# Splitting only the first of seven Fourier products a second time, and giving the projection's operands other buffers

## The chip, the cores and the metric

The kernel runs on one core of one Trainium2 chip. The metric is the device time of one execution in microseconds (us). The engines are named as in the profile: PE is the matrix engine (its weight loads are listed apart as PEld), DVE the vector engine, ACT the scalar engine, POOL the general engine, SP the engine that here issues all transfers between the chip's memory (DRAM) and its buffers (SBUF). PSUM is the memory that matmuls write to, in banks of 128x512 numbers. Each engine and the SP queue work through their instructions in a fixed order; an instruction whose semaphores are not there yet holds up all that stand behind it on that engine.

## The reference

Two independent results stand side by side in the output, both in fp32:

```python
# A: attention with 32 heads of width 32, S = 2048, D = 1024
qkv = x @ wqkv                      # (2048, 1024) @ (1024, 3072)
p = softmax(q @ k^T * 32 ** -0.5)   # per head
a = concat_heads(p @ v) @ wo        # the projection: (2048, 1024) @ (1024, 1024)
# B: Fourier mixing, real part of a two-dimensional transform
u, w = x @ dft_hid_re.T, x @ dft_hid_im.T
b = dft_seq_re @ u - dft_seq_im @ w
out = concatenate([a, b], axis=-1)
```

The kernel may take B in the other order, first over the sequence with the two 2048x2048 matrices (`ct`), then over the hidden dimension (`wd`): the first of these is the "first Fourier stage", `dense1`, the second is `dense2`.

## The kernel before

**Four dense stages and an attention.** The dense stages are the QKV product, `dense1`, `dense2` and the projection (`project`). Each saves multiplications by the scheme of Strassen and Winograd: a product of 2x2 blocks is had from seven block products instead of eight, at the price of sums and differences of operands beforehand and of results afterwards. The seven are numbered 1 to 7. For accuracy every fp32 operand is cut into a high and a low part of a faster format (`halves`: a cast `h`, then a subtraction for `l`), and each term costs three matmuls: hi by hi, lo by hi, hi by lo. One such matmul has 128x128 weights and moves 512 columns.

**dense1.** Its seven products come in the order `OUTER`, each over a quarter of the contraction. A product that is not split (`simple`) has 4x4 blocks of the result with 8 terms of three matmuls each, 384 matmuls; the stationary operand (from `xb`, 8 pieces) is loaded once and held, the moving one (from `ct`, 8 pieces) anew for each of four columns `n`. A product in `SPLIT` is cut into seven once more (`split`): 7 products of 4 blocks with 4 terms, 336 matmuls, but with more sums on DVE and POOL, operands that are written to DRAM and read back (`w_d`), and four tiles of accumulators, buffers 16 to 19. The unsplit products use these four buffers for half of the held pieces. Before, products 1, 2 and 3 are split.

**Operands.** `fetch` loads a quarter of an operand into a ring of six tiles `raw`, a second one into a ring of four tiles `g`, and adds or subtracts on POOL or DVE; a sum that is wanted again is stored. `moving` then makes the two halves in one of the numbered buffers (`slot`): 0 to 11 rotate through all dense stages, 12 to 15 and 20 to 27 belong to the projection once the attention's tiles are given up (`op_pool`), 16 to 19 hold accumulators or held pieces. `CR` is a ring of four tiles `c`, for earlier results that are read back to be added to.

**The order of the work.** A planner in the kernel (class `Plan` and the loop at the end) writes down the order of every engine ahead of time, by costs of its own. The matmuls of the dense stages are a list of fills that PE takes between those of the attention: scores twice per head (`psS`, L1536, for the row maxima and sums; `psT`, L1661, transposed, for the weights) and the product with V (`pd<-pt,vt`, L1691, four narrow matmuls side by side). PE takes a fill if nothing of the attention can run, or if the share of the fills that has been paid is not above the share of the attention that is done:

```python
TO_PAY = sum(x[3] for x in fills[: FILL - RES])       # a fill of a split product counts HEAVY = 1.5
if fill is not None and (not ok or (not first and left <= HB) or paid / TO_PAY <= done / ATT):
```

So the fills are spread over the attention such that the last of `dense2` are left when it ends. While a split product runs, and in the projection, ACT may make the casts as well (`spare[0]`).

**The end.** When the last head is done, its result goes to DRAM (`o_d<-ot`). `behind()` makes buffers 12 to 15 and 20 to 27 wait for the results of all heads, and so do the loads into the rings that `project` uses. Its seven products follow in the order 1, 7, 2, 6, 5, 3, 4, with 8 blocks of 4 terms each (96 matmuls); blocks 0 to 3 of the result use the moving operand `A[p, 0, c]` as stationary one (`J0`), blocks 4 to 7 `A[p, 1, c]` (`J1`), and `wo` is `B[p, c]`. `WHERE` says in which buffers they lie.

Of the kernel before, what the change touches and what calls it, by code (L numbers as in the profile page):

```python
# [8 lines left out]
F32 = mybir.dt.float32  # L9
# [215 lines left out]
def kernel(  # L225
# [38 lines left out]
    def slot(i, shape, dt=F32R):  # L264
        if i < 12:
            return big.tile(shape, dt, name=f"slot{i}", tag=f"slot{i}")
        if i < 16 and "pt2" in late:
            return op_pool().tile(shape, dt, name=f"slot{i}", tag=f"slot{i}")
        if i < 16:
            att()  # L270
            return late["low"].tile(shape, dt, name=f"slot{i}", tag=f"slot{i}")
        if i < 20:
            return run.tile(shape, dt, name=f"slot{i}", tag=f"slot{i}")
        if i < 28:
            op_pool()
            return late["oph"].tile(shape, dt, name=f"slot{i}")
        return vph.tile(shape, dt, name=f"slot{i}")

    parts = ctx.enter_context(tc.tile_pool(name="parts", bufs=1, side="right", reuse_waits="tile"))
# [12 lines left out]
    run = ctx.enter_context(tc.tile_pool(name="run", bufs=1, side="right", reuse_waits="tile"))  # L294
    qk0 = tc.alloc_tile_pool(name="qk0", bufs=1, side="right")
    QS, KS, QX = [qk0.tile([P, S], F32R, name="qs0")], [qk0.tile([P, S], F32R, name="ks0")], []
# [82 lines left out]
    ADD = 0.68  # L379
    SPLIT = (1, 2, 3)  # L380
    HEAVY = 1.5
# [67 lines left out]
    slots = [[] for _ in range(40)]  # L449

    def take_slot(i):
        old, slots[i] = slots[i], []
        return old, slots[i]
# [7 lines left out]
    class Kept:  # L461


        def __init__(self, get):
            self.get, self.made, self.users = get, None, []

    def fetch(shape, terms, store=None, keep=None):

        box = {}
        raws, seconds, tile_of, gate = where[0]  # L470
        rank = seq()
        sign, *first = terms[0]
        loaded = len(first) == 2
        if len(terms) == 1 and not loaded:
# [12 lines left out]
        last = None  # L487
        if loaded:
            last = op("SP", ISSUE, lambda: nc.sync.dma_start(dest(), first[0]), old + first[1] + gate, [users], rank, 256, raws if keep is None else None)
            old = []  # L490
        for sign, *term in terms[1:]:
            other = {}
            if len(term) == 2:
                gold, gusers = seconds.take()

                def load(src=term[0], other=other):
                    other["q"] = tile_of(shape, "g", len(seconds.users))
                    nc.sync.dma_start(other["q"], src)

                q = op("SP", ISSUE, load, gold + term[1] + gate, [gusers], rank, 256, seconds)  # L500
            else:
                other["k"], q, gusers = term[0], term[0].made, term[0].users

            def add(e, sign=sign, other=other, a=None if last is not None else first[0]):
                return (nc.gpsimd if e == "POOL" else nc.vector).tensor_tensor(  # L505
                    out=dest(), in0=dest() if a is None else a.get(), in1=other["q"] if "q" in other else other["k"].get(), op=ALU.add if sign > 0 else ALU.subtract)

            last = op("POOL", SUB, add, old + [first[0].made if last is None else last, q], [users, gusers] + ([first[0].users] if last is None else []),
                      rank, 0, raws if keep is None and last is None else None, other=("DVE", ADD, 20 + rank), two=True)
            old = []  # L510
        if keep is not None:
            keep.made = last
# [80 lines left out]
    class Acc:  # L593
# [5 lines left out]
        def at(self):  # L599
            return self.get()[:, self.half]  # L600
# [564 lines left out]

    OUTER = (1, 5, 2, 6, 7, 4, 3)
    WITHIN = (1, 2, 5, 6, 7, 3, 4)
    DONE_IN = {2: (0, 0), 7: (1, 1), 3: (0, 1), 4: (1, 0)}

    def outer(p, X, Y, to, wrote, neg):  # L1170
# [51 lines left out]
        return finish  # L1222

    def dense1():
        s4 = [[[] for _ in range(2)] for _ in range(4)]
# [11 lines left out]
        cq = lambda e, s, n: (ct[e, s, :, n * NB : n * NB + NB], [])  # L1237
        step = [0]

# [3 lines left out]
        def simple(p):  # L1243
# [11 lines left out]
            for n in range(4):  # L1255
# [15 lines left out]
                for m in range(4):  # L1271
# [4 lines left out]
                    if p == 7 and 3 in SPLIT and m % 2:  # L1276
                        i, k = divmod(2 * n + m // 2, 2)
                        fetch([P, 4, P], [(1, *xq(i, 8 + 4 * k)), (-1, s2_d[i][k], s2[i][k])], (s4_d[i][k], s4[i][k]))

        def split(i):  # L1280
            def base_a(m, k):
# [11 lines left out]
            at = lambda *k: (w_d[k], w[k])  # L1293
            x, y = accs(16) + accs(17), accs(18) + accs(19)
            for j in WITHIN:
                z = step[0]
                step[0] += 1
                A, M = [], {}
                for n in range(2):
                    A.append(piece(split_a(j, lambda r, k: base_a(2 * r + n, k), at(5, n), at(6, n)), at(j, n) if j in (5, 6) else None))  # L1300
                    for c in range(4):
                        M[n, c] = moving((8 * z + 4 * n + c) % 12, split_b(j, lambda k, e: base_b(4 * k + c, 2 * e + n), at(5, n, c), at(6, n, c)),
                                         at(j, n, c) if j in (5, 6) else None)
                for n in range(2):
# [41 lines left out]
    def dense2():  # L1346
# [9 lines left out]
        def load_ab(step, k):  # L1356
            p = ORDER[step]
            AB[step, k] = moving((8 * step + k) % 12, moving_terms(p, lambda r, e: (wd[r, k, :, e * NB : e * NB + NB], []), (t2_d[k], t2[k])),
                                 (t2_d[k], t2[k]) if p == 6 else None)
# [31 lines left out]
    def op_pool():  # L1391
        if "op" not in late:
            late["pt2"].release()
            att().release()
            qk0.release()
            late["atl"].release()
# [4 lines left out]
    def behind():  # L1401

        over.extend(o for h in o_st for o in h)
        for i in (*range(12, 16), *range(20, 28)):
            slots[i] = list(over)
# [5 lines left out]
    def project():  # L1411
# [15 lines left out]
        def b_terms(p, c):  # L1427
# [326 lines left out]
    dense2()  # L1754
    behind()
    project()


# [135 lines left out]
```

## Time and profile before

| | before |
|---|---|
| median of 3 runs | 2948.45 us (2947.95 to 2951.28) |
| the profiled execution | 2951.01 us; its span, first to last instruction, 2949.2 us |
| PE busy | 2919.6 us (99%), 14778 matmuls |
| DVE / ACT / POOL busy | 2311.3 (78%) / 2308.5 (78%) / 1188.9 us (40%) |
| transfers | 665.10 MB, mean 226 GB/s; SP's transfers take 69.5% of the 16 DMA engines' time |
| mean granted PE clock | 0.998 |

A trace's row for a group gives the line, the engine, the operation, and output <- inputs by the program's names. A matmul's record is longer than the step from one to the next (a mean of 390 ns, a step of under 230), since matmuls are pipelined; so the busy share of PE says little, and the count of matmuls in a stretch says more. A row of a table by stretches gives from:to, the length, busy time and count (x) of PE, PEld, DVE, ACT and POOL, then the granted PE clock, the mean busy share of the DMA engines and what they moved in GB/s. A product with V is recorded as two matmuls.

### The profile page before, as it was taken

The numbers are of one execution on the slowest core, as the hardware profiler recorded it, in microseconds if no ns is written. First come the engines' busy times: TensorE is split into PE (matmuls) and PEld (weight loads), VectorE is DVE, ScalarE is ACT, GpSimd is POOL, SyncE is SP. The second block draws the span as 40 slices with busy tenths as digits, with TensorE's granted clock in tenths as the row PEclk, the third lists the DMA queues.
The fourth block names the chain that finished last, engine by engine and source line by source line (L and its number), as shares of the span: only waits on it lengthen the run. The fifth ranks groups of instructions, "written<-read, shape, count | busy, mean of one in ns | idle before, by whom it ended". The sixth has DMA issues, their size and how long they took to land.

```text
span 2949.2 us, 46415 instructions
## 1 busy us (share of the span) xinstructions
PE 2919.6 (99%) x14778; PEld 2117.7 (72%) x14778; DVE 2311.3 (78%) x3127; ACT 2308.5 (78%) x4387; POOL 1188.9 (40%) x929
## 2 busy tenths in 40 slices
PE   9999999999999999999999999999999999999999
PEld 7887777777767677666777777777676677777677
DVE  7778888788888867988777787778877887876385
ACT  5347888888888888889888888898888888887431
POOL 2223335222366622676435342247512664342042
PEclk9999999999999999999999999999999999999999
DMA  9975668676697964989979775468734875663463
GB/s 345 370 239 179 206 189 276 213 239 222 229 294 239 324 199 146 294 256 323 307 234 289 227 235 171 147 197 273 226 101 149 283 231 183 189 189 117 161 207 125
DMA packets 460799, 665.10 MB, mean 226 GB/s; under 512 B 117486, under 2 KB 152046, under 8 KB 460430
## 3 DMA queue, kind: packets, MB, share of 16 engines
q1 hardware_dynamic: 460556, 662.14, 69.5%
q8 instruction: 119, 1.95, 0.3%
q14 instruction: 124, 1.02, 0.1%
HBM read 470.06 MB, written 191.91 MB: 224 GB/s over the span
## 4 chain that ended last, share of the span: by engine, by line
PE 58%; DMA 3%; DVE 2%; ACT 2%; issue 1%; POOL 1%; SPq 0%; DVEq 0%; POOLq 0%; ACTq 0%
PE pd L419 26%; PE psT L1661 10%; PE pd L1691 10%; PE psS L1536 9%; PE psT L419 3%; ACT psS L1545 2%; DMA raw<-in_ct 1%; DVE negm L1542 1%; DVE slot L526 0%; DMA g<-in_xb 0%; ACT pt L1668 0%; DMA g<-t_d 0%; POOL raw L505 0%; DVE slot L529 0%; DMA ks<-qk_d 0%
## 5 line engine op out<-in xcount | busy, mean ns | idle before, releaser
L1542 DVE TENSOR_REDUCE negm<-psS 128x1 f32<-128x1024 f32 x1024 | 1241.4, 1220 | 231.4 <-PE psS L1536 220.2
L1545 ACT ACTIVATE psS<-psS,negm 128x1024 f32<-128x1024 f32 x1024 | 1231.1, 1202 | 76.6 <-DVE negm L1542 75.0
L1668 ACT ACTIVATE pt<-psT 128x512 f32<-128x512 f32 x1656 | 1001.3, 703 | 257.1 <-PE psT L1661 235.3
L419 PE MATMUL pd<-slot,h 128*128 128x512 f32 x2784 | 952.9, 390 | 2.3 <-POOL slot L529 2.1
L1661 PE MATMUL psT<-qs,ks 128*128 128x512 f32 x2048 | 798.0, 395 | 4.1 <-ACT pt L1668 3.9
L505 POOL TENSOR_TENSOR raw<-raw,g 128x512 f32<-128x512 f32 x367 | 476.0, 1305 | 436.2 <-issue 63.1
L529 POOL TENSOR_TENSOR slot<-raw,slot 128x512 fp32r<-128x512 f32 x290 | 374.0, 1297 | 680.0 <-DVE slot L529 199.2
L419 PEld LDWEIGHTS pd<-slot,h 128*128 128x128 f32 x2784 | 523.0, 188 | 110.8 <-POOL slot L529 3.7
L419 PE MATMUL pd<-slot,l 128*128 128x512 f32 x1392 | 543.5, 390 | 1.9 <-DVE l L529 1.6
L1661 PEld LDWEIGHTS psT<-qs,ks 128*128 128x128 f32 x2048 | 382.1, 188 | 158.8 <-issue 44.4
L1536 PE MATMUL psS<-ks,qs 128*128 128x512 f32 x1552 | 476.0, 392 | 7.0 <-ACT psS L1545 7.0
L419 PE MATMUL pd<-slot,slot 128*128 128x512 f32 x1536 | 420.2, 389 | 0.0
L1691 PE MATMUL pd<-pt,vt 128*32 128x512 f32 x3312 | 408.2, 594 | 0.0
L1536 PEld LDWEIGHTS psS<-ks,qs 128*128 128x128 f32 x1552 | 288.2, 188 | 76.9 <-ACT psS L1545 17.4
L419 PEld LDWEIGHTS pd<-slot,slot 128*128 128x128 f32 x1536 | 288.5, 188 | 59.9
L1545 ACT ACTIVATION_READ_ACCUMULATOR psS<-psS,negm 128x1 f32 x1024 | 328.8, 321 | 0.0
L419 PEld LDWEIGHTS pd<-slot,l 128*128 128x128 f32 x1392 | 261.6, 188 | 57.1 <-DVE l L529 2.0
L1668 ACT ACTIVATE ptm<-psT 128x512 f32<-128x512 f32 x392 | 241.8, 710 | 43.8 <-PE psT L1661 40.6
L1691 PEld LDWEIGHTS pd<-pt,vt 128*32 128x32 f32 x3312 | 108.5, 110 | 231.4 <-issue 219.3
L529 POOL TENSOR_TENSOR l<-raw,h 128x512 fp32r<-128x512 f32 x120 | 155.2, 1293 | 276.7 <-PE psT L1661 79.3
L526 DVE CAST slot<-raw 128x512 fp32r<-128x512 f32 x375 | 192.0, 531 | 8.4 <-POOL raw L505 7.6
L1536 PE MATMUL psS<-ks,qx 128*128 128x512 f32 x496 | 150.5, 394 | 3.4 <-ACT psS L1545 3.4
(140 smaller groups left out, 2047.4 us busy)
## 6 DMA issues: line engine op xcount, KB each, us to landing
raw<-in_ct SPq DMA_DIRECT2D x240, 256.0 KB
g<-in_ct SPq DMA_DIRECT2D x168, 256.0 KB
raw<-ut_d SPq DMA_DIRECT2D x112, 256.0 KB
qk_d<-e SPq DMA_DIRECT2D x52, 512.0 KB
qs<-qk_d SPq DMA_DIRECT2D x128, 192.0 KB
ks<-qk_d SPq DMA_DIRECT2D x128, 192.0 KB
c<-xx_d SPq DMA_DIRECT2D x80, 256.0 KB
c<-u_d SPq DMA_DIRECT2D x72, 256.0 KB
```

Of the source, the lines that this page charges most:

```text
L419: nc.tensor.matmul(box["ps"], a[1]((a[0].hi, a[0].lo)[u]()), b[1]((b[0].hi, b[0].lo)[v]()), start=k == 0, stop=k == n - 1)
L505: return (nc.gpsimd if e == "POOL" else nc.vector).tensor_tensor(out=dest(), in0=dest() if a is None else a.get(), in1=other["q"] if "q" i ...
L526: return nc.vector.tensor_copy(hi(), raw())
L529: return (nc.gpsimd if e == "POOL" else nc.vector).tensor_tensor(out=lo(), in0=raw(), in1=f(hi()), op=ALU.subtract)
L1536: nc.tensor.matmul(p[:, i * NB : i * NB + NB], (QX[0] if own else QS[h % 2])[:, qt * P : qt * P + P], KS[h % 2][:, c * 1024 + i * NB : c * ...
L1542: nc.vector.tensor_reduce(out=ST["negm"][:, c, qt : qt + 1], in_=box["p"], axis=AX.X, op=ALU.max, negate=True)
L1545: nc.scalar.activation(box["p"], box["p"], AF.Exp, bias=ST["negm"][:, c, qt : qt + 1], accum_out=ST["sums"][:, c, qt : qt + 1])
L1661: nc.tensor.matmul(box["p"], KS[h % 2][:, t * P : t * P + P], QS[h % 2][:, j * NB : j * NB + NB], start=True, stop=True)
L1668: nc.scalar.activation(box["t"], box["p"], AF.Exp)
L1691: nc.tensor.matmul(po["p"][j * DH : j * DH + DH, :], VT[h][:, k, :], box["t"], start=(k == t0), stop=(k == t), tile_position=(0, j * DH),)
```

## The change

Only product 1 of `dense1` is split; products 2 and 3 become `simple`. The order of the seven products puts 2 ahead of 5. In product 1, for one of the two halves of the columns, four tiles that are needed by inner products 1, 5, 6 and 4 stay in SBUF, in the four tiles of `CR`: each is loaded with a quarter of `ct` and then turned in place into t = q01 - t, t = q11 - t, t = t - q10, instead of being stored and read back; `fetch` learns to take the operands of a subtraction the other way round. The buffers 24 to 27 are no longer given out when the attention's tiles are given up: they become the halves of two tiles that take the place of `qs0` and `ks0`, Q and K of the even heads, which are free when head 30 has had its last scores. Products of the projection are laid out anew (`WHERE`), such that `B[1, c]` goes to the bank of 0 to 11 that `dense2` leaves free and `A[1, 0, c]` to 24 to 27; both are asked for ahead of `behind()`. In the planner's sum `FILL` and in its weights the split products 2 and 3 drop out.

```diff
-        if i < 28:
+        if i < 24:
             op_pool()
             return late["oph"].tile(shape, dt, name=f"slot{i}")
+        if i < 28:
+            return both(i, dt)[:, i % 2 * 2 : i % 2 * 2 + 2]
...
+    def both(i, dt):
+        n, turn = i // 2, turns[i]
+        if whole_of.get(n, (None, None))[0] != turn:
+            whole_of[n] = turn, qk0.tile([P, 4, NB], dt, name=f"both{n}", tag=("qs0", "ks0")[n % 2])
...
-    SPLIT = (1, 2, 3)
+    SPLIT = (1,)
...
     def take_slot(i):
+        if 24 <= i < 28:
+            if i % 2 == 0:
+                first[i] = slots[i] + slots[i + 1]
+            old, slots[i] = first[i - i % 2], []
+            return old, slots[i]
...
-    OUTER = (1, 5, 2, 6, 7, 4, 3)
+    OUTER = (1,2,5,6,7,4,3)
...
+            own = {(1, c): stays() for c in range(4)} if i == 1 else {}
...
+                        t = own.get((n, c))
+                        if t is not None and j in (1, 5, 6, 4):
+                            terms = {1: lambda: [(1, *q(0, 0))], 5: lambda: [(-1, t), (1, *q(0, 1))], 6: lambda: [(-1, t), (1, *q(1, 1))], 4: lambda: [(1, t), (-1, *q(1, 0))]}[j]()
+                            M[n, c] = moving((8 * z + 4 * n + c) % 12, terms, None, t)
...
+        g = [(8 * (steps[0] + 7) + 4 * k) % 12 for k in range(3)]
         WHERE = {
-            1: ([20, 24], 0), 7: ([4, 8], 20), 2: ([0, 4], 24), 6: ([8, 0], 20),
-            5: ([4, 8], 24), 3: ([0, 4], 20), 4: ([8, 0], 24),
+            1: ([24, 20], g[0]), 7: ([g[1], g[2]], 24), 2: ([g[0], g[1]], 20), 6: ([g[2], g[0]], 24),
+            5: ([g[1], g[2]], 20), 3: ([g[0], g[1]], 24), 4: ([g[2], g[0]], 20),
         }
...
+        for i in range(24, 28):
+            slots[i] = [Tops[H - 2][-1], Sops[H - 2][-1]]
         load_b(1)
-        load_a(1, J0 + J1)
+        load_a(1, J0)
+        behind()
+        load_a(1, J1)
```

The built programs show what this does to the order. Counted over the whole program, PE has 96 matmuls more (two products with 384 instead of 336), SP issues 2624 transfers instead of 2840, POOL has 775 instructions instead of 934, DVE 3061 instead of 3129, ACT 3320 instead of 3365.

**The end of the first product, on SP.** Before, loads, second operands (`g`) and stores of sums (`s_d`, `t_d`) for product 5 are issued while the results of product 1 (`xx_d`) are written:

```order
L489 DMA raw<-in_ct 128x512
L514 DMA s_d_0_534<-raw 128x512
L498 DMA g<-in_ct 128x512
L489 DMA raw<-in_xb 128x512
L970 DMA xx_d_0_1_438<-e 128x512
L514 DMA t_d_0_542<-raw 128x512
L498 DMA g<-in_xb 128x512
L514 DMA t_d_1_543<-raw 128x512
```

Now single loads for product 2 stand there:

```order
L994 DMA xx_d_0_1_454<-e 128x512
L511 DMA raw<-in_xb 128x512
L1205 DMA c<-xx_d_0_1_454 128x512
L511 DMA raw<-in_xb 128x512
L994 DMA xx_d_1_1_442<-e 128x512
L511 DMA raw<-in_xb 128x512
L324 DMA ks_333<-qk_d_3_85 96x512
```

The second operands and the stores of product 5 have moved behind product 2, one product further on.

**The end of the attention, on PE.** Here the last block of `dense2` (`slot,h` and `slot,l`) is followed by the projection's first product. Before:

```order
L419 MATMUL psT<-slot_30505,h 128x512
L419 MATMUL psT<-slot_30505,l 128x512
L419 MATMUL psT<-slot_30505,h 128x512
L419 MATMUL psT<-slot_31205,slot_31235 128x512 x3
L419 MATMUL psT<-slot_31211,slot_31257 128x512 x3
L419 MATMUL psT<-slot_31219,slot_31262 128x512 x3
```

Now:

```order
L433 MATMUL psT<-slot_29912,h 128x512
L433 MATMUL psT<-slot_29912,l 128x512
L433 MATMUL psT<-slot_29912,h 128x512
L433 MATMUL psT<-slot_30363,both_30532 128x512 x3
L433 MATMUL psT<-slot_30386,both_30532 128x512 x3
L433 MATMUL psT<-slot_30467,both_30589 128x512 x3
```

The first product reads the new tiles; between the last product with V and this place stand 53 matmuls of `dense2` before, and 91 now.

**The same place on SP.** Before, all of the projection's loads stand behind the store of the last head's result:

```order
L1731 DMA o_d_200<-ot 128x512
L970 DMA out<-e 128x512
L489 DMA raw<-in_wo 128x512 x4
L489 DMA raw<-o_d_193 128x512
L970 DMA out<-e 128x512
```

Now two of the four loads of `wo` stand ahead of it, and the others right behind:

```order
L511 DMA raw<-in_wo 128x512
L994 DMA out<-e 128x512
L1006 DMA c<-u_d_601 128x512
L511 DMA raw<-in_wo 128x512
L1781 DMA o_d_200<-ot 128x512
L511 DMA raw<-in_wo 128x512
L994 DMA out<-e 128x512
L511 DMA raw<-o_d_193 128x512
```

Of the 36 transfers for the projection's first two products, 34 are still issued after the attention.

More of the change, by code (lines that the diff above doesn't have):

```diff
@@ L488, in fetch @@
         if loaded:
-            last = op("SP", ISSUE, lambda: nc.sync.dma_start(dest(), first[0]), old + first[1] + gate, [users], rank, 256, raws if keep is None else None)
+            last = op("SP", ISSUE, lambda: nc.sync.dma_start(dest(), first[0]), old + first[1] + gate, [users], rank, 256, raws if keep is None else keep.ring)
             old = []
@@ L511, in fetch @@
         if keep is not None:
-            keep.made = last
+            keep.made, keep.ring = last, None
         if store is not None:
@@ L1278, in simple, with stays, get @@
                         fetch([P, 4, P], [(1, *xq(i, 8 + 4 * k)), (-1, s2_d[i][k], s2[i][k])], (s4_d[i][k], s4[i][k]))
+        def stays():
+            box = {}
+            def get():
+                if "t" not in box:
+                    box["t"] = sums_pool().tile([P, NB], F32, name="c", tag="c", bufs=NCR)
+                return box["t"]
+            k = Kept(get)
+            old, k.users = CR.take()
+            k.users.extend(old)
+            k.ring = CR
+            return k
         def split(i):
```

30 lines of the change are left out of this document (19 added, 11 removed).

## The prediction

> **What bounds the kernel now.** I read the page's first block, then the chain that ended last, then the span cut at the places where one dense product ends and the next begins. The page says PE:
>
> ```profile
> span 2949.2 us, 46415 instructions
> PE 2919.6 (99%) x14778; PEld 2117.7 (72%) x14778; DVE 2311.3 (78%) x3127; ACT 2308.5 (78%) x4387; POOL 1188.9 (40%) x929
> ```
>
> A busy PE need not be a fast one, so I want the price of a matmul at full pace. The chain near the end gives it (start, length, what):
>
> ```profile
> 2763.95 7.00 PE pd L1691 x64
> 2770.95 6.80 PE pd L419 x29
> ...
> 2779.90 4.59 DMA raw<-o_d
> ...
> 2789.67 5.47 PE pd L419 x24
> 2795.14 5.44 PE psT L419 x24
> ...
> 2808.78 0.69 DVE slot L995
> 2809.47 1.92 DVE slot L529 x3
> ...
> 2813.42 4.06 PE psT L419 x9
> 2817.48 5.44 PE pd L419 x24
> ```
>
> Twenty-four matmuls take 5.44 us, 0.2267 us each; 64 records of the product with V take 7.00 us, 0.1094 each. With these two prices any stretch says how much it lost. The stretches below end where the count of dense matmuls (second table, line L419) reaches a product's 336 or 384; in order they are QKV, products 1 (split), 5, 2 (split), 6, 7, 4, 3 (split), dense2, projection. The third table counts the records with V.
>
> ```profile
> 0.00:782.20 782.20, 780.01 (x3831) 584.78 (x3832) 623.67 (x857) 575.59 (x1079) 252.66 (x200) 1.00 0.73 245
> 782.20:961.80 179.60, 177.76 (x924) 125.36 (x923) 157.74 (x222) 156.90 (x301) 108.90 (x86) 0.99 0.83 266
> 961.80:1167.00 205.20, 199.10 (x1025) 139.44 (x1024) 153.04 (x190) 170.73 (x327) 72.06 (x57) 1.00 0.69 223
> 1167.00:1341.70 174.70, 171.34 (x869) 119.71 (x868) 154.44 (x200) 156.17 (x300) 119.83 (x95) 1.00 0.86 273
> 1341.70:1548.30 206.60, 203.91 (x1042) 142.75 (x1041) 166.09 (x227) 176.80 (x340) 93.23 (x73) 1.00 0.88 286
> 1548.30:1744.30 196.00, 195.79 (x1024) 141.43 (x1023) 151.25 (x200) 167.32 (x321) 82.44 (x64) 1.00 0.78 249
> 1744.30:1940.40 196.10, 196.10 (x1025) 141.65 (x1025) 146.01 (x198) 168.30 (x326) 51.80 (x40) 1.00 0.56 170
> 1940.40:2125.60 185.20, 181.85 (x947) 125.54 (x946) 154.10 (x207) 163.53 (x316) 117.70 (x94) 1.00 0.79 248
> 2125.60:2783.00 657.40, 656.49 (x3429) 469.29 (x3429) 487.33 (x666) 529.87 (x1014) 238.46 (x185) 1.00 0.56 173
> 2783.00:2949.20 166.20, 157.25 (x673) 127.74 (x671) 117.64 (x168) 43.34 (x72) 51.83 (x40) 0.98 0.54 187
> ```
>
> ```profile
> 961.80:1167.00 205.20, 113.55 (x385) 71.74 (x384) 1.00 0.69 223
> 1167.00:1341.70 174.70, 99.55 (x337) 63.03 (x336) 1.00 0.86 273
> ```
>
> ```profile
> 782.20:961.80 179.60, 33.86 (x304) 9.26 (x304) 0.99 0.83 266
> 961.80:1167.00 205.20, 35.37 (x320) 9.89 (x320) 1.00 0.69 223
> 1167.00:1341.70 174.70, 28.30 (x256) 7.91 (x256) 1.00 0.86 273
> 1548.30:1744.30 196.00, 35.37 (x320) 9.89 (x320) 1.00 0.78 249
> 1744.30:1940.40 196.10, 35.37 (x320) 9.89 (x320) 1.00 0.56 170
> 1940.40:2125.60 185.20, 35.37 (x320) 9.89 (x320) 1.00 0.79 248
> 2125.60:2783.00 657.40, 120.25 (x1088) 33.62 (x1088) 1.00 0.56 173
> ```
>
> Worked once: product 5 has 1025 - 320 = 705 full matmuls, 159.8 us, and 320 records with V, 35.0 us; it lasts 205.2, so it loses 10.4 us. In the same way product 1 loses 5.8, product 2 7.7, product 6 7.9 (320 records with V, as its neighbours), product 3 8.1, dense2 7.7 in its 657 us. Products 7 and 4, unsplit and between unsplit ones, lose 1.4 and 1.3: that is the calm rate. So splitting saves 48 matmuls, 10.9 us, and the split products or the product behind them give most of it back.
>
> Where in product 5? In its first 60 us; two of PE's waits and the chain name it:
>
> ```profile
> PE pd L419 <- POOL slot L529: 2.1, 1, 2.1
> PE pd L419 <- DVE l L529: 1.6, 1, 1.6
> ```
>
> ```profile
> 957.73 4.91 DMA raw<-in_ct
> 962.66 6.42 DMA g<-in_xb
> ...
> 973.79 6.25 DMA g<-in_xb
> ```
>
> ```profile
> 970.00:980.00 10.00, 7.99 (x33) 6.07 (x34) 8.59 (x9) 8.21 (x17) 5.72 (x5) 1.00 0.97 293
> 1340.00:1350.00 10.00, 8.97 (x37) 6.23 (x36) 8.31 (x11) 10.00 (x21) 7.88 (x8) 1.00 0.98 296
> 2780.00:2790.00 10.00, 8.38 (x30) 6.20 (x29) 6.70 (x11) 4.75 (x8) 0.00 (x0) 0.83 0.83 268
> 2800.00:2810.00 10.00, 8.74 (x39) 6.91 (x37) 7.24 (x12) 4.79 (x9) 5.09 (x4) 1.00 0.99 344
> ```
>
> The DMA engines are at 0.97 of their time, a 256 KB load takes over 6 us, and PE waits for sums made from it. Product 6 begins alike (second row, 0.98).
>
> **The change part by part.** The profiled execution took 2951.01 us, 1.8 more than its span; the median of the runs, 2948.45, is 2.6 lower. The sum is made against 2951.0.
>
> *Matmuls.* Two products with 384 instead of 336: 96 x 0.2267 = +21.8 us. PE takes them in sequence with all else, so they lie on the path in full; nothing hides them.
>
> *Products 2 and 3 unsplit.* Each now has, for every column, eight moving pieces from one load (for 2 and for 3 alike no sum), and 8 held pieces, single for 2 and a difference for 3. That is less work on DVE, POOL and SP than products 7 and 4 have, which lose 1.4 and 1.3. Bounds: no gain at all (0) and the calm rate, -6.3 for product 2 and -6.8 for 3. The stage of 4 is nearest, so I take close to the end: losses of 1.7 and 1.6, -6.0 and -6.5.
>
> *Product 5 behind a light product 2.* Its first column is the same: 16 loads and 8 stores for the held pieces, 16 and 8 for the moving ones. Counted in the order between neighbouring loads of K (about a quarter of a head), SP moves 7.3, 4.1, 8.3, 2.6, 7.0 and 2.8 MB where product 5 begins, against 5.5, 7.8, 6.0, 7.5, 5.7 and 5.2 before: the worst three together 19.7 against 21.3, the six 32.1 against 37.7. The peak remains, the queue behind it drains sooner. Bounds: 0 and -9.0 (calm); I take the middle, -5.4.
>
> *Product 6 behind 5 instead of behind a split one.* Its own transfers stay, but nothing of an inner product is in flight when it begins, and counted in the order PE does 79 pairs of scores (`psS`) during this product instead of 84, so that fewer stretches hold attention alone. Bounds 0 and -6.5; I take -4.9.
>
> *The four tiles that stay.* Per tile three loads of stored sums or quarters and two stores fall away, 20 transfers of 256 KB in product 1. Its loss is 5.8; bounds +2 (a transfer of 6.4 us held up once at the ring `CR`, less what other fills cover) and -4.4; I take -0.5. New waits: `CR` serves no reloads until inner product 4 has read the tiles, and behind a load that waits for it on SP stand K and Q of the attention. At zero, since product 1 reloads nothing through `CR`, and product 2 needs its first reload only at the end of a block of 24 matmuls, 5.4 us.
>
> *dense2.* Loses 7.7 with a split product ahead of it and will start calmer; bounds +1 and -2; -0.5. QKV, products 7 and 4: 0.
>
> *The end.* From 2770.95 to 2817.48 PE does 53 matmuls of dense2, 96 of the projection's first product and 12 of its second: 161 x 0.2267 = 36.5 us in 46.5. Ten are lost, to o_d and then to sums for the second product (the DVE rows). Now 91 matmuls of dense2 stand behind the attention, so the first product is due 20.6 us after it and the second 42.4, instead of 12.0 and 33.8. First operands were there at 2789.67 or 18.7 us, the second's between 42.5 and 46.5; with 34 transfers instead of 36 in the way these come 1.5 us sooner (0.76 each at the 344 GB/s of the last row above). The 38 extra matmuls are not new work, they were only moved behind the attention. So the first stall goes and the second shrinks to some 2 us. Bounds -4 and -10; I take -7.6. The halves of 24 to 27 share a tile, so product 7's casts wait for all four blocks of `J0`; nothing is paid, as the four blocks of `J1` cover it with 10.9 us.
>
> The granted clock belongs in this term: in 2780:2790 PE idled 1.6 us and the clock fell to 0.83, worth 1.7 us more. The Trainium skill ("TensorE: Matmul & The Clock Gate", What's actually happening) has the clock halve after an idle window of about 3.4 us; by that the 2 us that I leave could cost no clock, by the row they can cost 1.7 more and the term would be -5.9. The measurement decides: a shorter idle was enough.
>
> Sum: 21.8 - 6.0 - 6.5 - 5.4 - 4.9 - 0.5 - 0.5 - 7.6 = -9.6 us. 2951.0 becomes 2941.4, and as the median lies 2.6 lower, 2939.
>
> **The rivals.**
>
> *The burst moves with product 5.* Its first column has the same 48 transfers, 12.6 MB, and product 6 behind it the same again. If their stalls come from these transfers alone, 10.4 and 7.9 stay: -9.6 + 5.4 + 4.9 = +0.7, a median of 2949. For it: the peak of three neighbours is hardly lower. Against: product 5 lasted through five such intervals in a row, now two. On this side also a page: the Trainium skill ("DMA: Bandwidth & Descriptors", Measured) has a lone core reach 425 GB/s with 16 MB, so that 293 to 344 would be no ceiling of bytes and fewer bytes would not help. The share of 0.97 in the row above speaks against that reading.
>
> *Slower: the attention, not the splitting, makes the stalls.* In 1340:1350 ACT is busy 10.00 of 10 us while PE loses a tenth: PE ran ahead and waited for exponentials. Should unsplit products meet the same limit, the losses of 2, 5, 6 and 3 stay, and only the end is repaid: 21.8 - 7.6 - 1.0 = +13.2, a median of 2962. It decides once an unsplit product needs ACT for more of its time than there is; in product 4 ACT is busy 168.3 of 196.1 us with no loss, and the order gives 79 to 81 pairs of scores to each unsplit product, as before.
>
> *The early buffers come no earlier.* All four loads of A for `J0` still stand behind the last head's store. If the first operands are late in spite of the 20.6 us, the end keeps its ten: -2.0, median 2946.5.
>
> *Better.* Products 5, 6 and 1 fall to the calm rate and the end loses nothing: -6.3 - 6.8 - 9.0 - 6.5 - 4.4 - 2 - 10 + 21.8 = -23, median 2925 at the farthest.
>
> **How the numbers follow.** 2948.45 us times 0.2% is 5.9 us, about what a measurement tells from no change; faster means under 2942.6. My forecast, 2929 to 2945, has 0.58; better than that 0.09; the moved burst 0.16; the early buffers in vain 0.09; the attention as the limit 0.08. The forecast's upper end (0.05) and two rivals are no change: 0.05 + 0.16 + 0.09 = 0.30, less 0.05 for halfway cases of the moved burst that still end under 2942.6, 0.25. Faster: 0.53 + 0.09 + 0.05 = 0.67. Slower 0.08. The range for 8 in 10 leaves out the attention case, the upper half of the moved burst and the farthest gains: 2929 to 2949.
>
> **What would show it.** Matmuls 14874. Products 2 and 3 last 96 x 0.2267 / 2 = 10.9 us more than their matmuls before, but lose under 2 us each by the count. Product 5's first 60 us lose half of what they lost, still with DMA shares above 0.9 for some 30 us. PE's waits on ACT (`psS`) shrink. Behind the last product with V PE runs 139 matmuls without a break, and no clock row at 0.83 follows before the second product. The forecast is wrong if product 5 or 6 loses 8 us again, or if a new wait of SP on `c` tiles holds up K.

## The result, and the profile after

| | before | after |
|---|---|---|
| median | 2949.74 us (2947.95 to 2951.28, 4 runs) | 2933.26 us (2932.89 to 2936.67, 4 runs) |
| ratio | | 0.9947, 95% interval 0.9933 to 0.9961 |
| the profiled execution | 2951.01 us, span 2949.2 | 2933.28 us, span 2931.5 |
| transfers | 665.10 MB | 608.43 MB |

The kernel is 16.5 us faster, where 9.6 were forecast: 2933 for 2939, inside the range of 2929 to 2949. (The four runs of the kernel before are the three ahead of the prediction and one more.) A second set of runs of the changed kernel (the label `after_again` below) gave 2934.61 us and 0.9953 (0.9941 to 0.9966), 12.5 us under its own runs of the kernel before.

The first lines of the page of after; 96 matmuls more, as forecast, and 159 instructions fewer on POOL:

```profile
span 2931.5 us, 45842 instructions
PE 2920.6 (100%) x14874; PEld 2140.3 (73%) x14874; DVE 2251.2 (77%) x3059; ACT 2283.5 (78%) x4342; POOL 987.0 (34%) x770
```

The span of after cut at the same places, in its own order: QKV, products 1 (split), 2, 5, 6, 7, 4, 3, dense2, projection. The columns are those of the prediction's table.

```profile
0.00:783.90 783.90, 779.96 (x3832) 584.10 (x3833) 619.44 (x852) 575.46 (x1079) 250.35 (x198) 1.00 0.74 245
783.90:949.00 165.10, 164.15 (x840) 118.93 (x839) 144.39 (x208) 151.83 (x292) 106.15 (x84) 1.00 0.78 243
949.00:1144.40 195.40, 195.12 (x1020) 140.16 (x1019) 144.01 (x190) 165.35 (x320) 48.60 (x38) 1.00 0.57 172
1144.40:1341.80 197.40, 197.38 (x1029) 142.33 (x1028) 146.09 (x191) 169.28 (x327) 77.14 (x60) 1.00 0.72 232
1341.80:1536.60 194.80, 194.80 (x1020) 140.73 (x1019) 150.84 (x204) 166.03 (x320) 75.54 (x60) 1.00 0.81 267
1536.60:1731.90 195.30, 195.30 (x1023) 141.13 (x1022) 154.27 (x206) 166.76 (x321) 61.68 (x49) 1.00 0.70 218
1731.90:1928.40 196.50, 196.50 (x1028) 142.04 (x1027) 148.81 (x202) 168.06 (x326) 57.02 (x44) 1.00 0.58 176
1928.40:2125.10 196.70, 196.47 (x1026) 141.47 (x1025) 140.44 (x183) 168.75 (x325) 32.55 (x26) 1.00 0.43 126
2125.10:2774.70 649.60, 648.16 (x3397) 463.65 (x3396) 484.98 (x672) 513.35 (x982) 222.45 (x173) 1.00 0.58 177
2774.70:2931.50 156.80, 152.79 (x673) 125.80 (x671) 117.88 (x159) 38.57 (x64) 55.52 (x43) 1.00 0.51 177
```

The records with V in three of them (product 1 has 240 now, each of the six unsplit products 320, dense2 1088):

```profile
783.90:949.00 165.10, 26.79 (x240) 7.29 (x240) 1.00 0.78 243
949.00:1144.40 195.40, 35.37 (x320) 9.89 (x320) 1.00 0.57 172
2125.10:2774.70 649.60, 120.25 (x1088) 33.61 (x1088) 1.00 0.58 177
```

With the prediction's prices (0.2267 us for a matmul, 0.1094 for a record with V) each row says what it lost. Product 5: 709 x 0.2267 + 320 x 0.1094 = 195.7 of 197.4 us, 1.7 lost. Of every projection's window 4.1 us lie behind its last matmul and are no loss; they are taken off below.

| stage | lost before | lost after | change | forecast |
|---|---|---|---|---|
| 96 matmuls more | | | +21.8 | +21.8 |
| 2 (was split) | 7.7 | 1.7 | -6.0 | -6.0 |
| 3 (was split) | 8.1 | 1.6 | -6.5 | -6.5 |
| 5 | 10.4 | 1.7 | -8.7 | -5.4 |
| 6 | 7.9 | 1.1 | -6.8 | -4.9 |
| 1 (split) | 5.8 | 2.8 | -3.0 | -0.5 |
| dense2 | 7.7 | 7.1 | -0.6 | -0.5 |
| the end (projection) | 9.5 | 0.1 | -9.4 | -7.6 |
| 7 and 4 | 2.7 | 1.9 | -0.8 | 0 |
| QKV | 13.2 | 14.7 | +1.5 | 0 |

The sum is -18.5, the spans differ by 17.7: a matmul that straddles a cut is counted in both rows, three of them more after than before, 0.7 us.

The chain at the end of after. Behind the product with V PE runs 187 matmuls (67 + 36 + 24 + 24 + 24 + 12) before the first sum comes late (139 were forecast), and the block of 24 in which it does takes 5.92 us (2793.88 to 2799.80) instead of 5.44:

```profile
2746.97 7.00 PE pd L1741 x64
2753.97 15.41 PE pd L433 x67
2769.38 8.18 PE psT L433 x36
2777.56 5.44 PE pd L433 x24
2783.00 5.44 PE psT L433 x24
2788.44 5.44 PE pd L433 x24
2793.88 2.73 PE psT L433 x12
...
2797.33 0.52 DVE both L553
...
2797.90 1.90 PE psT L433 x7
2799.80 5.46 PE pd L433 x24
```

### The profile page after: what moved, and what is told of

It reads as the page before. It is cut to its first block, busy times and chain, and to the rows that moved or that the text cites. A ratio compares the mean times of both kernels' runs of the same rounds, so it can differ in the third digit from the quotient of the medians.

```text
span 2931.5 us, 45842 instructions
## 1 busy us (share of the span) xinstructions
PE 2920.6 (100%) x14874; PEld 2140.3 (73%) x14874; DVE 2251.2 (77%) x3059; ACT 2283.5 (78%) x4342; POOL 987.0 (34%) x770
## 2 busy tenths in 40 slices
DMA packets 429690, 608.43 MB, mean 208 GB/s; under 512 B 114030, under 2 KB 148590, under 8 KB 429326
## 4 chain that ended last, share of the span: by engine, by line
PE 75%; ACT 1%; DVE 1%; DMA 0%; issue 0%; SPq 0%; POOL 0%; DVEq 0%; ACTq 0%
PE pd L433 34%; PE psT L1711 13%; PE pd L1741 12%; PE psS L1586 12%; PE psT L433 3%; ACT psS L1595 1%; DMA raw<-in_ct 0%; DVE negm L1592 0%; ACT pt L1718 0%; SPq L324 0%; DVE l L553 0%; DVE slot L553 0%; DVE h L550 0%; DVE slot L550 0%; POOL l L553 0%
## 5 line engine op out<-in xcount | busy, mean ns | idle before, releaser
L433 PE MATMUL pd<-slot,h 128*128 128x512 f32 x2592 | 881.3, 390 | 0.0
L553 POOL TENSOR_TENSOR slot<-raw,slot 128x512 fp32r<-128x512 f32 x251 | 323.1, 1293 | 931.1 <-DVE slot L550 539.2
L433 PEld LDWEIGHTS pd<-slot,h 128*128 128x128 f32 x2592 | 486.6, 188 | 101.0 <-issue 0.8
L530 POOL TENSOR_TENSOR raw<-raw,g 128x512 f32<-128x512 f32 x285 | 370.1, 1307 | 434.3 <-DMA raw<-in_ct 67.6
L433 PE MATMUL pd<-slot,l 128*128 128x512 f32 x1296 | 504.8, 390 | 0.0
L433 PE MATMUL pd<-slot,slot 128*128 128x512 f32 x1752 | 494.0, 389 | 0.0
L433 PEld LDWEIGHTS pd<-slot,slot 128*128 128x128 f32 x1752 | 329.0, 188 | 68.4
L433 PEld LDWEIGHTS pd<-slot,l 128*128 128x128 f32 x1296 | 243.3, 188 | 50.2
L553 POOL TENSOR_TENSOR l<-raw,h 128x512 fp32r<-128x512 f32 x94 | 121.4, 1292 | 206.4 <-PE psT L1711 78.4
L550 DVE CAST slot<-raw 128x512 fp32r<-128x512 f32 x365 | 165.7, 475 | 6.9 <-DMA raw<-in_wo 3.1
```

Source lines behind the costliest of these rows:

```text
L433: nc.tensor.matmul(box["ps"], a[1]((a[0].hi, a[0].lo)[u]()), b[1]((b[0].hi, b[0].lo)[v]()), start=k == 0, stop=k == n - 1)
L550: return nc.vector.tensor_copy(hi(), raw())
```

## The experiments

"Lost" is always counted as above. Each comparison is with runs of the kernel before on the same chip. Lines of kernels made from after have after's numbers. Where an expectation gives another loss for a run already made (8.0 for product 5 with 5 second, 10.2 for the end of `split13`), the count by the rows below, 7.5 and 9.7, holds.

### Anchor: the changed kernel again

> The changed kernel once more, on the chip of the next three, so that these can be compared with it directly: 0.9947 of the kernel before, as measured.

2934.61 us, 0.9953; span 2931.3, product 5 lost 1.2, the end 0.2, QKV 14.6. Between these two profiles of the same kernel no stage's loss differs by more than half a microsecond.

### Product 5 behind the split product again

```diff
-    OUTER = (1,2,5,6,7,4,3)
+    OUTER = (1, 5, 2, 6, 7, 4, 3)
```

> The changed kernel with the order of the products put back to 1, 5, 2, 6, 7, 4, 3: product 5, with its 48 transfers in the first column, again directly behind the split product 1. Theory one: its stall is back, 10.4 instead of 1.6 us by the count of matmuls, so 2942 us, with PE waiting for sums on POOL and DVE in its first 60 us and the DMA engines above 0.95. Rival: the stall left because product 1 moves less with the four tiles that stay; then 2933 to 2935.

2937.47 us, ratio 0.9974 (0.9963 to 0.9984), between the two forecasts; span 2934.4, 2.9 us above after's. Product 5 lost 7.5 instead of 1.7; of the other stages none lost more than in after but product 1 (3.0 for 2.8), and QKV, product 2 and dense2 lost 1.2, 0.8 and 0.8 less. Product 5's row, and the 20 us that cost most:

```profile
948.00:1150.60 202.60, 199.68 (x1026) 143.02 (x1026) 154.20 (x203) 168.80 (x325) 68.77 (x54) 0.98 0.72 231
960.00:970.00 10.00, 7.08 (x30) 5.12 (x28) 7.08 (x8) 7.91 (x16) 4.42 (x4) 0.94 0.98 319
970.00:980.00 10.00, 10.00 (x33) 7.96 (x34) 6.84 (x11) 8.00 (x15) 3.84 (x3) 0.72 0.97 304
```

In the last row PE is busy 10.00 of 10 us and does 33 matmuls, not 44: the granted clock was 0.72. In the 10 us before it PE was idle for 2.9, waiting for a sum, and the chain says for what:

```profile
955.70 4.55 DMA t_d<-raw
...
960.33 5.50 DMA raw<-in_xb
...
965.85 1.41 DVE raw L530
...
967.33 1.26 POOL raw L530
968.59 1.23 POOL l L553
...
969.87 0.79 PE pd L433
```

A store of product 5's sums, then a load into the tile that the store had read, two sums, PE. So the stores are suspect, in two ways: as traffic, or because each keeps a tile of `raw` until it has left. Two kernels tell these apart. The first takes the stores away:

```diff
-            keep_a = {5: lambda m, k: (s1_d[m][k], s1[m][k]), 6: ...
+            keep_a = {6: ...
-            keep_b = {5: lambda n, c: (t1_d[n][c], t1[n][c]), 6: ...
+            keep_b = {6: ...
```

> The changed kernel with 5 as second product, and with nothing stored by 5: product 6 reads input quarters where it read the stored sums, so its result is another. Product 5's first column has 32 transfers instead of 48, with the same sums, the same casts and the same buffers; product 6 keeps its 48. With the stores, product 5 lost 8.0 us by the count and the kernel took 2937.5 us (before in that session 2946.3). Theory (bytes: what queues behind the split product's end are transfers, and the stores are a third of them): product 5 loses 2 to 4 us, the kernel is 4 to 6 us faster than with the stores, about 13.5 us faster than the kernel before. Rival (the chain of two loads and a sum, or the accumulators' buffers 16 to 19 that come free late): product 5 loses 7 to 9 as it did, the kernel is about 9 us faster than the kernel before.

2934.04 us, 0.9956 (0.9943 to 0.9968), between the two forecasts, so the time alone does not decide; QKV happened to lose 17.0 here against 13.5. The stage decides: product 5 lost 2.3, so the stores are behind the stall, as traffic or by their tiles.

The second puts a copy of the same size in each store's place, one that holds no tile:

```diff
+            keep_a = {5: lambda m, k: (s1_d[m][k], s1[m][k], xq(4 + m, 4 * k)[0]), 6: ...
...
-            ... nc.sync.dma_start(store[0], dest()), [last], [users], ...
+            ... nc.sync.dma_start(store[0], store[2] if len(store) > 2 else dest()), [last], [] if len(store) > 2 else [users], ...
```

> The kernel with 5 second and nothing stored by it, but in the place of each store that fell away a copy of 256 KB from DRAM to DRAM, with the same wait on the sum; it does not read a tile of the ring raw, and nobody reads what it writes. PE's order is the same as with the real stores, and SP's is nearly so. As in the run without stores product 6 reads input quarters, so its result is another. Theory (bytes: the transfers queue, 48 of them again): product 5 loses 6 to 9 us as with the real stores, the kernel is about 9 us faster than the kernel before. Rival (the ring: a store holds its tile raw until it has left, and the next load waits for the tile; in the chain of the run with real stores a store of 4.55 us stands ahead of a load of 5.50): product 5 loses 2 to 4 us as without stores, the kernel is 12 to 13 us faster than the kernel before.

2943.78 us, 0.9985 (0.9976 to 0.9994), and product 5 lost 11.9, more than with the real stores. So traffic alone, though of another kind than the stores, makes a stall here without any tile being held. It is not shown that the ring adds nothing when the stores are real: in the chain above the load starts only when a store has left. That copies cost more than stores was not expected; they read DRAM as well as write it. PE now waits for a load itself:

```profile
PE pd L433 <- DMA raw<-in_xb: 4.6, 1, 4.6
```

How much traffic is too much? The 60 us ahead of product 5's first matmul and the first 60 us behind it, in after and with 5 second:

```profile
1084.40:1144.40 60.00, 59.72 (x295) 44.52 (x294) 49.11 (x67) 53.49 (x105) 24.66 (x19) 1.00 0.77 236
1144.40:1204.40 60.00, 59.98 (x329) 41.10 (x328) 48.99 (x69) 48.60 (x94) 27.86 (x22) 1.00 0.87 283
```

```profile
888.00:948.00 60.00, 60.00 (x298) 45.52 (x297) 53.05 (x75) 56.74 (x109) 38.33 (x31) 1.00 0.80 253
948.00:1008.00 60.00, 57.08 (x302) 38.06 (x302) 48.09 (x67) 43.52 (x84) 25.71 (x21) 0.94 0.97 317
```

In 120 us after moved 60 x (236 + 283) = 31.1 MB, the kernel with 5 second 34.2. The same rows, read for product 5 or 6 of other runs (some of them described further below):

| kernel, product | MB in 120 us | DMA share in its first 60 us | lost |
|---|---|---|---|
| `five_second_nostore`, 5 | 29.8 | 0.83 | 2.3 |
| after, 5 | 31.1 | 0.87 | 1.7 |
| after, 6 | 31.9 | 0.96 | 1.1 |
| `five_second_copy`, 5 | 32.6 | 0.94 | 11.9 |
| `three_split`, 6 | 32.9 | 0.97 | 3.0 |
| `before_no_act`, 5 | 33.1 | 0.94 | 11.4 |
| before, 5 | 33.8 | 0.97 | 10.4 |
| `five_second`, 5 | 34.2 | 0.97 | 7.5 |
| `three_split`, 5 | 35.1 | 0.98 | 13.9 |
| `before_no_act`, 6 | 35.3 | 0.99 | 6.9 |
| before, 6 | 36.0 | 0.98 | 7.9 |

In all other runs products 5 and 6 moved at most 32.5 MB and lost at most 2.9. So, the copies aside, up to 32.9 MB cost at most 3.0 us and 33.1 MB and more cost 6.9 to 13.9, in no order of size. The share of the first 60 us alone does not tell the two groups apart: product 6 of after ran at 0.96 and PE idled 0.00 us in that time. The runs differ in more than their megabytes, so this is a pattern that they show, not a limit that one of them tested. It holds for 5 and 6 only: the split product 2 of before moved 24.1 MB and lost 7.7. What the split products themselves lose by was not tested.

### Three products split, the rest as in after

```diff
-    SPLIT = (1,)
+    SPLIT = (1, 2, 3)
```

> The changed kernel with products 1, 2 and 3 split again, and all else of the change kept (order 1, 2, 5, the four tiles that stay, the early buffers). It has 96 matmuls less than the changed kernel, 21.8 us at 0.2267. Theory one, that a stall comes where the operands of a split product meet those of the next one: product 2 loses 7.7 again, 5 behind it 10.4, 3 again 8.1, product 6 behind an unsplit 5 stays calm and the end stays whole; that gives back about 21 us, so 2933 us, the same as the changed kernel. Rival, that order, tiles and early buffers alone took the stalls away and unsplitting was not needed: none comes back, 2933 - 21.8 = 2911.

2955.19 us, 1.0031 (1.002 to 1.0042). Both expectations missed: with all else of the change kept, splitting 2 and 3 is slower than before. Two rows (product 5; the projection) and the wait at the end:

```profile
1124.60:1336.10 211.50, 205.10 (x1037) 143.26 (x1036) 160.27 (x205) 175.14 (x337) 88.66 (x69) 0.99 0.79 259
2771.90:2952.40 180.50, 164.10 (x738) 129.59 (x736) 119.35 (x172) 42.97 (x73) 44.02 (x34) 0.96 0.49 172
```

```profile
PE psT L433 <- ACT both L549: 10.9, 2, 9.7
```

Products 2 and 3, split as before, lost 4.7 and 4.6 (7.7 and 8.1 expected). Product 5 stands behind the split product 2 and lost 13.9; product 6, now behind the unsplit 5, lost 3.0 instead of 7.9. And the end lost 16.6, since in this order the last product with V comes 17 matmuls into the projection: no matmul of dense2 is left to cover its loads.

### Are the casts on ACT to blame?

In the kernel before, with the split products' casts kept off ACT:

```diff
-            spare[0] = p in SPLIT
+            spare[0] = False
```

> The kernel before, where only DVE makes the casts in the split products (ACT makes none there). The order then leaves 89 matmuls of dense2 behind the attention instead of 53. Theory one: the stalls at products 5, 2, 6 and 3 come from operands that arrive late and stay, about 30 us together; only the end gains its 7 to 9 us, so 2940 where the kernel before takes 2948. Rival: the casts on ACT hold up the exponentials and so make those stalls; then 20 us or more are gained, 2928.

2949.47 us, 1.0002 (0.9993 to 1.0011): neither forecast. The stalls of the split products and of 5 and 6 stay (1: 9.9, 5: 11.4, 2: 6.5, 6: 6.9, 3: 8.8), so the casts on ACT did not make them (though DVE, which makes these casts here, may hold up others in their place: product 1 lost 4.1 more than before). Nor do PE's waits for ACT's work on the scores go with the casts; they go with the change. In the kernel before, here, and in after:

```profile
PE psS L1536 <- ACT psS L1545: 10.3, 22, 1.1
```

```profile
PE psS L1536 <- ACT psS L1545: 12.7, 22, 1.7
```

```profile
PE psS L1586 <- ACT psS L1595: 2.2, 5, 1.1
```

But the planner, which books those casts on ACT, now has room for the attention earlier: 89 matmuls of dense2 are left behind it in the order instead of 53, and the end lost 4.2 instead of 9.5, without any early buffer.

### The four tiles that stay

```diff
-            own = {(1, c): stays() for c in range(4)} if i == 1 else {}
+            own = {}
```

> The changed kernel without the four tiles that stay: inner products 1, 5, 6 and 4 of product 1 load, store and read back as before, 20 transfers of 256 KB more in product 1. Theory one: product 1 loses 5.8 us again instead of 2.7, so 2936 us, and the transfers are what the tiles saved. Rival: the loss of product 1 had another cause (a cast on ACT that waits ahead of the exponentials), and nothing changes, 2933.

2938.55 us, 0.9971 (0.9961 to 0.9982), 4 us slower than the second set of after, which ran on another chip; the spans differ by 2.9. Product 1 lost 4.3 (after 2.8), where 5.8 were expected, product 5 2.9 (1.7), the end 3.5 (0.1). The first may be put down to the tiles; that the second comes from them too is not shown. The third is odd: 112 matmuls of dense2 stand behind the attention here, more cover than in after, and still PE stood for 1.9 us, and 3.41 us at half clock behind that cost 1.7 more. By the chain the load that PE's sum needed (`g<-o_d`, 4.46 us) was issued only at 2770.02, right behind a store of results (L994) that had waited for DVE. Why DVE came to it so late is left open.

### The end: early buffers or cover

First the early buffers are taken back; `behind()` comes before all loads, and 24 to 27 wait for all heads (with `behind()` ahead, ACT may cast these operands too and other rings hold them, so it is not the buffers alone):

```diff
+        behind()
+        for i in range(24, 28):
+            slots[i] = list(over)
         load_b(1)
         load_a(1, J0)
-        behind()
```

> The changed kernel with its layout of buffers, but the projection's first operands wait for the results of all heads again, as before. Theory one: with 91 matmuls of dense2 behind the attention instead of 53 the first product is due 20.6 us after it, and before the change its operands were there at 18.7, so most of the end's gain stays: 2 to 4 us come back, 2936. Rival: the early buffers made the whole gain of the end, 9 us come back, 2942. Other rival: they made none of it, 2933.

2935.47 us, 0.9961 (0.9947 to 0.9974). With the same 91 matmuls of cover the end lost 1.3 instead of 0.1, and dense2 8.2 instead of 7.1: with this much cover the early buffers are worth some 1 to 2 us.

Then the cover is taken away and the buffers stay, by splitting product 3 too (its casts on ACT delay the attention):

```diff
-    SPLIT = (1,)
+    SPLIT = (1, 3)
```

> The changed kernel with product 3 split as well: 48 matmuls less, 10.9 us. Theory one: product 3 loses 4.8 instead of 2.0 as in the kernel with three split ones, dense2 behind it some 4 us more, and with 19 matmuls of dense2 instead of 91 behind the attention the projection's first operands come too late by up to 14 us; so 6 to 10 us slower than the changed kernel, 2940. Rival: only the neighbours of a split product matter, not the cover at the end: 10.9 saved, 3 to 7 given back, 4 to 8 us faster, 2926.

2935.29 us, 0.9956 (0.9944 to 0.9969). Nineteen matmuls of dense2 are left as cover, and the end lost 9.7 with all its early buffers, as much as before. Product 3 lost 5.4. The third kernel splits 1 and 3 and lets ACT cast only in 1, which by the order leaves 67:

```diff
-            spare[0] = p in SPLIT
+            spare[0] = p == 1
```

> The changed kernel with product 3 split as well, where ACT makes casts only during product 1. By the order 67 matmuls of dense2 stand behind the last product with V, against 19 with casts on ACT during 3 and 91 in the changed kernel. Theory (the end is decided by how much of dense2 is left as cover): the projection loses 3 to 5 us instead of 10.2, product 3 loses 6 to 7, the sum is about 4 us less than with the casts and about 1 us less than the changed kernel: 14 to 17 us faster than the kernel before. Rival (without ACT product 3 loses what the end gains): no faster than the split of 1 and 3 with casts on ACT, 11 us under the kernel before.

2929.23 us, 0.9941 (0.9928 to 0.9955), 16.5 us under the kernel before. The end lost 4.0, product 3 7.1. Projections of the last three, and the worst 10 us of `split13`:

```profile
2775.70:2933.70 158.00, 153.35 (x673) 125.70 (x671) 114.49 (x158) 39.59 (x66) 53.18 (x41) 1.00 0.52 179
```

```profile
2766.30:2932.70 166.40, 156.78 (x673) 127.81 (x671) 117.93 (x167) 41.88 (x69) 49.23 (x38) 0.97 0.53 184
2790.00:2800.00 10.00, 5.88 (x12) 3.64 (x13) 8.25 (x14) 5.16 (x10) 1.04 (x1) 0.58 1.06 387
```

```profile
2767.80:2928.50 160.70, 155.14 (x673) 126.85 (x671) 117.08 (x162) 39.34 (x65) 54.40 (x42) 0.99 0.52 181
```

With 19, 67 and 91 matmuls of cover (4.3, 15.2 and 20.6 us) and early buffers the end lost 9.7, 4.0 and 0.1. All kernels that leave any cover, some of them from other sections:

| kernel | early buffers | cover | the end lost |
|---|---|---|---|
| `split13` | yes | 19 | 9.7 |
| before | no | 53 | 9.5 |
| `split13_na` | yes | 67 | 4.0 |
| `split13_na_o` | yes | 85 | 0.0 |
| `before_no_act` | no | 89 | 4.2 |
| after | yes | 91 | 0.1 |
| `late_end` | no | 91 | 1.3 |
| `no_kept` | yes | 112 | 3.5 |
| `split0` | yes | 139 | 0.5 |

So cover matters most, but it is not all: `no_kept` lost 3.5 with 112, and `before_no_act` and `late_end` differ by 2.9 at nearly the same cover. And early buffers are worth more where cover is short: before lost with 53 what `split13` lost with 19, and on a straight line between `split13` and `split13_na` 53 would lose 5.7 with them, an estimate. `split13_na` is the best kernel found. Its span is 3.0 us below after's, but its interval overlaps those of after, so that it beats after is likely and not settled.

### Is splitting product 1 still worth it, and would 3 be better placed?

```diff
-    SPLIT = (1,)
+    SPLIT = ()
```

> The changed kernel with no product split at all: 48 matmuls more, 10.9 us. Theory one: product 1 loses 1.5 instead of 3.1 us and the end, with 139 matmuls of dense2 behind the attention, nothing: 8 to 9 us slower than the changed kernel, 2941. Rival: a split product costs its whole gain wherever it stands, then within 2 us of the changed kernel.

2941.06 us, 0.9976 (0.9966 to 0.9986), 6.4 us slower than after on the same chip. The split of product 1 saves 10.9 us of matmuls and keeps 6.4.

`split13_na` with product 3 ahead of 4 instead of last:

```diff
-    OUTER = (1,2,5,6,7,4,3)
+    OUTER = (1,2,5,6,7,3,4)
```

> As the run before, with product 3 ahead of product 4 instead of last, so that an unsplit product follows it and not dense2. By the order 85 matmuls of dense2 stand behind the last product with V. Theory: the projection loses 1 to 2 us, product 3 and product 4 behind it 7 to 9 together, dense2 7 to 8; 10.9 us of matmuls saved against the changed kernel leave a gain of 2 to 4 us on it: 16 to 19 us faster than the kernel before. Rival (a product behind a split one pays back what the split saves, as 5 and 6 did): product 4 loses 6 to 8 instead of 1.5 and the kernel is no faster than the changed one, 12 to 14 us under the kernel before.

2934.44 us, 0.9955 (0.9942 to 0.9967). The end lost nothing, but 3 and 4 together lost 16.3 (11.7 and 4.6; the forecast had 7 to 9), with the clock at half for 3.41 us in product 3. The rival is nearer: what the split saves is paid back next to it, here already inside it.

## Why the prediction was right, and where its sizes were off

*Matmuls, products 2 and 3.* 14874 matmuls; 2 and 3 lost 1.7 and 1.6, as taken from the stage of product 4. These three terms came out to the tenth; for 2 and 3 that is partly luck, as `after_again` has 1.9 and 1.8.

*Product 5.* The middle between 0 and -9.0 was the step that failed; it went to the calm rate, -8.7. "The peak remains, the queue behind it drains sooner" is what the rows show (a share of 1.01 in 1170:1180), but it costs PE nothing. The forecast let the loss shrink with the megabytes; the table of the 120 us shows two groups instead, up to 3.0 us lost or 6.9 and more, and the change takes product 5 from 33.8 MB to 31.1. `five_second` shows that the place in the order makes 5.8 of the 8.7 us (7.5 for 1.7), 3.4 of these by the clock; where the other 2.9 (10.4 for 7.5) went was not tested. That traffic alone can make the stall, the kernel with copies shows; how much of it the ring of `raw` adds stays open.

```profile
1160.00:1170.00 10.00, 10.00 (x45) 8.26 (x44) 7.82 (x9) 10.00 (x21) 6.94 (x7) 1.00 0.86 254
1170.00:1180.00 10.00, 10.00 (x45) 8.26 (x44) 6.72 (x6) 10.00 (x21) 3.78 (x3) 1.00 1.01 382
```

*Product 6.* The same step, -6.8 for -4.9. `three_split` has it behind the unsplit 5 with 2 and 3 split, and it lost 3.0 there, 4.9 less than before: being behind a split product was most likely the larger part of its loss.

*Product 1.* -3.0 for -0.5. The tiles account for 1.0 to 1.5 (`no_kept` against the two sets of after, 3.3 and 2.8). Before, the clock was at half for 3.41 us from 847 us on, inside product 1, which costs 1.7; in after and in `no_kept` it is not there, so it is the likely rest. The feared wait at `CR` did not appear in the waits of PE.

*The end.* -9.4 for -7.6. The prediction left 2 us of stalls; 0.1 remained. Its main reason holds: without the early buffers (`late_end`) the end still loses 8.2 less than before, so the extra cover of dense2 does most of it. What it missed is that cover hangs on how far behind the attention is at the end, which the casts on ACT during split products decide; the change has such casts in product 1 only. The clock was counted once (1.7); before had two stretches of 3.41 us at half speed there, 3.4 us.

*QKV.* +1.5 with the same count of matmuls. Over the kernels made from after it lost 11.9 to 17.0. Why it scatters was not looked into, so the +1.5 is not explained.

*The rivals.* "The burst moves with product 5" had a cause that is enough for the stall (`five_second_nostore`, `five_second_copy`) and the result wrong, since behind a light product the same 48 transfers cost 1.7 us. "The attention, not the splitting" is refuted by product 5 in after, 0.02 us idle with ACT at 20.00 of 20 us in 1160:1180. PE's waits for ACT's work on the scores fell from 10.3 to 2.2 us, as the prediction's signs had it, and `before_no_act` shows that the casts on ACT are not what made these waits. "The early buffers come no earlier" was beside the point: without them, behind the same cover, the end lost 1.3. "Better" named the right stages; its farthest end of 2925 was not reached, as QKV and dense2 gave nothing.

## What to carry to other kernels

Where loads are near the limit of the DMA engines, what stands ahead of an operand-heavy stage can decide whether it stalls: here the same product lost 1.7 us behind a light stage and 7.5 behind a heavy one. Try a light stage between two heavy ones before changing either. For the tail, count the work in microseconds that is left behind the last dependency, and protect that cover from whatever delays the dependency; behind enough cover early buffers were worth little here. When a stage may fall to the calm rate or stay, do not take the middle by default: sum its megabytes, the stretch ahead of it included, and compare with stages of the same kernel whose loss is known.

## What the runs showed of the hardware

- The busy share of the DMA engines does not fix the rate. At shares of 0.97 the start of product 5 moved 293 to 323 GB/s and the first 75 us of the kernel before 344; at 1.06 (the view's share can pass 1) the projection's loads of `split13` moved 387. The Trainium skill ("DMA: Bandwidth & Descriptors", Measured) has 425 GB/s for a lone core with 16 MB; 387 comes near it, which points to the mix of transfers at product 5 and not to a ceiling of bytes. Which of them is dear was not measured, beyond that product 5 lost more with copies from DRAM to DRAM than with stores (11.9 against 7.5). Nor does a high share mean that PE starves: product 6 of after began with 60 us at 0.96 and lost 1.1.
- By the clock record of the traces all stretches at half clock within the work lasted a multiple of 3.413 us: 3.41 (in the kernel before from 847.3, 2786.1 and 2813.4 us on), 6.83 (`five_second`), 10.24 (`split13`), 13.65 (`three_split`). The Trainium skill ("TensorE: Matmul & The Clock Gate", What's actually happening) speaks of an idle window of about 3.4 us; the multiples agree with that, but PE need not be idle for a whole one: 1.8 us of idle time brought the 3.41 us from 847.3 on, and 2.9 us in `five_second` brought 6.83 us at half clock, worth 3.4 us, nearly half of the 7.5 that its product 5 lost. Nor does idle time of this length always bring it: the waits of 2.1 and 1.6 us at the start of product 5 in the kernel before cost no clock.
